# Spatial-reduction attention with a mixture of adapters: gated activations of 27 chunks turned by DMA, query columns in another order

## The chip, the cores and the metric

The kernel runs on one core of a Trainium2 chip. The metric is the device time of one execution in microseconds. A core has five engines that run side by side and wait for each other by semaphores: TensorE (PE in the profile; its weight loads are PEld), VectorE (DVE), ScalarE (ACT), GpSimd (POOL) and SyncE (SP). SyncE does no arithmetic here: it issues DMAs, one after the other, and waits before each for what that DMA needs. Casting DMAs are issued by GpSimd. Each engine works through its own instructions in program order, so an instruction that waits holds up all that follow on its engine.

## The reference

Queries `q` (4 batches of 12288 rows of 128 channels) attend to keys that are averages of 4 x 4 patches of `kv`, so 768 keys a batch, and keys and values are the same. Each output row then goes through 2 of 8 rank-16 adapters.

```python
kv_pool = kv.reshape(B, H // r, r, W // r, r, C).mean(axis=(2, 4))
kv_flat = kv_pool.reshape(B, -1, C) @ w_sr
k = v = kv_flat
s = scale * (q @ k.transpose(0, 2, 1))
a = np.exp(s - s.max(-1, keepdims=True))
a /= a.sum(-1, keepdims=True) + 1e-09
x = a @ v
...
logits = x @ w_gate
topk = np.argpartition(-logits, K, axis=1)[:, :K]   # K = 2
...
out = x + sum over the two chosen experts e of  w_e * ((x @ A[e]) @ B[e])
```

The second softmax is over the two chosen logits. The kernel computes all eight adapters at once as one 128 x 128 down-projection (8 experts of rank 16), multiplies the 128 activations by the gate of their expert, and applies one 128 x 128 up-projection.

## The kernel before

**Chunks and slots.** The 49152 queries are cut into 96 chunks of 512 (24 a batch), each of four pieces of 128 rows. Four chunks form a group. The first chunks are ordered by a list written out by hand (`opening`). From `k = 8` on a Python loop writes one slot per pass (line 547), and `keep` holds every engine to that order. In slot k from 13 on TensorE does three score pairs (`unit` calls `scores`) for chunk k and the attention of chunk k - 1, while chunk k - 2 is normalised. An older chunk goes through the adapters: it enters in some slot t (`enter[t]`; `kx`) with its transposes and down-projection, has its gated activations turned one slot later (`kh`), and gets its up-projection and its result two slots after it entered (`ku`).

**A slot on TensorE,** in order: the first score pair; `transposes`, which turns the four pieces of normalised rows of the entering chunk (`xn`) and the four pieces of gated activations of the chunk before (`hg`) into one PSUM tile `tt_ps`; the second pair; `up` (`d_ps`) of the chunk that is two slots on; six attention matmuls of the first piece (`acc`); the third pair; `down` (`h_ps`); in some slots (`rest`) a step of the next batch's keys and values (`kpT_ps`, `v_ps`, `kfT_ps`); 18 attention matmuls of the three other pieces.

**VectorE in a slot:** reciprocal of the softmax sums (`rinv`), normalisation (`xn`), copy of `tt_ps` to `tts`, sum of up-projection and rows (`osb`), `max` for the routing, gating (`gate`, writes `hg`), and the copies of `rest`. ScalarE takes the exponential of each score pair (`em`) and a tanh for the gates. GpSimd computes the gates (`over`, `gw`), adds up the patches of the next batch (`kvr`) and issues the casts of the queries.

**Buffers.** PSUM has eight banks. `ps_s` has two tiles of two banks for the score pairs, `ps_a` one tile of two banks for the attention, `ps_m` two tiles of one bank, which `tt_ps`, `d_ps`, `h_ps` and the tiles of `rest` take in turn. A tile is given out again when everything that reads its last contents is done. In SBUF, `xn` has a ring of six pairs of chunks, results eight buffers (`osb`), `tts` and `hg` three each.

**Queries.** From group 2 on GpSimd casts a group to bf16 in DRAM (`cast_q`), and SyncE loads it transposed (`load_qT`), group g in slot 4g - 6 for most. Row 16p + j of a group sits in partition p of the output; the transposed group has columns in the order (j, p), so that chunk m of a group is the j from 4m to 4m + 3. Groups 0 and 1 are turned by TensorE (`turn_q`).

**The last part.** The chunks from `TURN` = 68 up to `SOLO` = 90 (`by_dma`) have both their normalised rows and their gated activations turned by DMA from SyncE (`narrow`, `strip`, `turn_dma`), without TensorE; the last six chunks stand in a tail written out by hand.

Of the kernel before, what the change touches and what calls it, by code (L numbers as in the profile page):

```python
# [11 lines left out]
BF16 = mybir.dt.bfloat16  # L12
U16 = mybir.dt.uint16
FP16 = mybir.dt.float16
AF = mybir.ActivationFunctionType
# [5 lines left out]
def kernel(  # L21
# [10 lines left out]
    nc = tc.nc  # L32
    P = 128
    B, N, C = q.tensor.shape
# [20 lines left out]
    ppool = ctx.enter_context(tc.tile_pool(name="ppool", bufs=8))  # L55
    xpool = ctx.enter_context(tc.tile_pool(name="xpool", bufs=1))
    rpool = ctx.enter_context(tc.tile_pool(name="rpool", bufs=4))
    gpool = ctx.enter_context(tc.tile_pool(name="gpool", bufs=6))
    run = ctx.enter_context(tc.tile_pool(name="run", bufs=3))
    opool = ctx.enter_context(tc.tile_pool(name="opool", bufs=8))  # L60
    qdram = ctx.enter_context(tc.tile_pool(name="qdram", bufs=1, space=bass.MemoryType.DRAM))
    ps_s = ctx.enter_context(tc.tile_pool(name="ps_s", bufs=2, space=bass.MemoryType.PSUM))
# [3 lines left out]
    keep = tc.keep_in_program_order  # L66

    def mm(*a, **k):
        return keep(nc.tensor.matmul(*a, **k))  # L69
# [5 lines left out]
    NG = N // GT  # L75
    q_bf, qT, kvr, spare = {}, {}, {}, {}

    def cast_q(g):
        t = qdram.tile([GT, C], BF16, tag=f"q{g}", name=f"qbf{g}")
        keep(nc.gpsimd.dma_start(t, q[g // NG, (g % NG) * GT:(g % NG + 1) * GT]))  # L80
        q_bf[g] = t

    def load_qT(g):
        if g < B * NG - GC:
            t = qpool.tile([P, GT], BF16, tag="qT", name="qT")
        else:
            if "q" not in spare:
                spare["q"] = kvpool.tile([P, 4, 2, 4 * C], FP32, tag="kvr", name="qTs")
            t = spare["q"][:, g % GC].rearrange("p x c -> p (x c)").bitcast(BF16)
        keep(nc.sync.dma_start(t.rearrange("c (j p) -> c j p", p=P),  # L90
                               q_bf[g].rearrange("(p j) c -> p (j c)", p=P), transpose=True))
        qT[g] = t


# [191 lines left out]
    def scores(k, r):  # L286
        b = k // NB
        if k not in em:
            em[k] = ppool.tile([P, J, T], FP16, tag="em", name="em")
        rhs = qT[k // GC][:, (k % GC) * T:(k % GC + 1) * T]  # L290
        ps = ps_s.tile([P, 2, T], FP32, tag="sg", name="sg")
        for i in range(2):
            mm(ps[:, i], kfT[b][:, 2 * r + i], rhs, start=True, stop=True)
        keep(nc.scalar.activation(em[k][:, 2 * r:2 * r + 2], ps, AF.Exp, bias=0.0, scale=scale))  # L294

    def attend(k, s):
        b = k // NB
        if s == 0:
            acc[k] = ps_a.tile([P, S, 256], FP32, tag="acc", name="acc")
        o = acc[k][:, s, 0:VE]  # L300
        for j in range(J):
            mm(o, em[k][:, j, s * P:(s + 1) * P], vx[b][:, j, 0:VE], start=(j == 0),
               stop=(j == J - 1))

    def attend_part(k, r):
        if r == 0:
            acc[k] = ps_a.tile([P, S, 256], FP32, tag="acc", name="acc")
        for s in range(S):
            for j in (2 * r, 2 * r + 1):
                mm(acc[k][:, s, 0:VE], em[k][:, j, s * P:(s + 1) * P], vx[k // NB][:, j, 0:VE],  # L310
                   start=(j == 0 and s % 2 == 0), stop=(j == J - 1 and s % 2 == 1))

    def normalize(k):
# [91 lines left out]
    def turn_dma(t, *what):  # L405
# [3 lines left out]
        for i, (d, k) in enumerate(what):  # L409
            d[k] = strip(t, 1)[:, lo + i]  # L410

    def down(k):
        hp[k] = mtile([P, S, P], name="h_ps")
        for s in range(S):
            mm(hp[k][:, s], xT[k][:, s], a_bf, start=(s == 0), stop=(s == S - 1))

    def gate(k, into=None):
        k0, m = first[k], k - first[k]
        hg[k] = run.tile([P, S, P], BF16, tag="hg", name="hg") if into is None else into
        keep(nc.vector.tensor_tensor(  # L420
            hg[k].rearrange("p s (e r) -> p (s e) r", e=E),
            hp[k].rearrange("p s (e r) -> p (s e) r", e=E),
            gw[k0][:, m * S:(m + 1) * S].rearrange("p s e -> p (s e)")
            .unsqueeze(2).broadcast_to([P, S * E, RK]), op=ALU.mult))

    def up(k):
        dp[k] = mtile([P, S, C], name="d_ps")
        for s in range(S):
            mm(dp[k][:, s], hgT[k][:, s], b_bf, start=(s == 0), stop=(s == S - 1))

    def finish(k):
        osb = opool.tile([P, S, C], FP32, tag="osb", name="osb")
        keep(nc.vector.tensor_tensor(osb, dp[k], xn[k][:, :, 0:C], op=ALU.add))  # L433
        keep(nc.sync.dma_start(
            out[k // GC * GT:(k // GC + 1) * GT].rearrange("(p j) c -> p j c", p=P)
            [:, k % GC * S:(k % GC + 1) * S], osb))
        for d in (em, acc, xn, xT, hgT, hp, hg, dp):
            d.pop(k, None)

# [25 lines left out]
    loads.update({61: 20, 63: 21, 64: 18, 65: 22, 66: 19, 67: 23})  # L465
    assert len(casts) == B * NG - 4

    def begin(k):
        nonlocal sums, rest
        b, i = divmod(k, NB)  # L470
        g = k // GC
        if k in loads:
            load_qT(loads[k])
        if k in casts:
            cast_q(4 + casts.index(k))
        if b + 1 < B:
            lo = 3 if b == 0 else 0
            if i == lo:
                sums, rest = prepare(b + 1, nc.gpsimd)
                sums = sum(sums, [])  # L480
            if lo <= i < 12 + lo:
                load_kv(b + 1, (i - lo) // 4, (i - lo) % 4, None)
        if k == 7:
            for _ in range(2):
                sums.pop(0)()
# [12 lines left out]
    while left:  # L498
        can = [k for k in left if ready[k] <= t]
        enter[t] = can[:2] if t == SOLO + 2 else can[:1]  # L500
        left = [k for k in left if k not in enter[t]]
        t += 1

    kh, ku, kd, kdone = [], [], [], []
    engines = {"DVE": nc.vector, "ACT": nc.scalar, "POOL": nc.gpsimd}
# [41 lines left out]
    for k in range(k1, NCHUNK):  # L547
        b, i = divmod(k, NB)
        ka = att.get(k, [])
        kx = enter.get(k, [])  # L550
        begin(k)

        def after_norm(kn):
            top(kn)
# [2 lines left out]

        kn = [n for n in att.get(k - 1, []) if normed[n] == k]
        unit()
        if kx and not kd and all(x_ in by_dma for x_ in kx):  # L560
            down(kx[0])
            todo = []
            for n in kn:
                normalize(n)
                if n in by_dma:
                    narrow(n, k)
                    todo = [(xT, n)]
            tanhs()
# [22 lines left out]
            kh, ku = kx, kh  # L591
            continue
        tanhs()
        for x_ in kd:
# [1 line left out]
        for n in kn:  # L596
            normalize(n)
            if n in by_dma:
                narrow(n, k)
                turn_dma(k, (xT, n))  # L600
        px, ph = ([c for c in ks if c not in by_dma] for ks in (kx, kh))
        pairs = [(px[j] if j < len(px) else None, ph[j] if j < len(ph) else None)
                 for j in range(max(len(px), len(ph)))]
        for x_, h_ in pairs[:1]:
# [71 lines left out]
    def part(k, o, js):  # L676
        for s in range(S):
            for j in js:
                mm(o[:, s, 0:VE], em[k][:, j, s * P:(s + 1) * P], vx[k // NB][:, j, 0:VE],
                   start=(j == 0 and s % 2 == 0), stop=(j == J - 1 and s % 2 == 1))  # L680

    def wide(o):
# [9 lines left out]
        for s in range(S):  # L692
            mm(o[:, s], hgT[k][:, s], b_bf, start=(s == 0), stop=(s == S - 1))

    def dest(k):
        return out[k // GC * GT:(k // GC + 1) * GT].rearrange("(p j) c -> p j c", p=P)[
            :, k % GC * S:(k % GC + 1) * S]

    def add_here(k, lo, hi, queue):
        osb = opool.tile([P, S, C], FP32, tag="osb", name="osb")[:, 0:hi - lo]  # L700
        keep(nc.vector.tensor_tensor(osb, dp[k][:, lo:hi], xn[k][:, lo:hi, 0:C], op=ALU.add))
        keep(queue.dma_start(dest(k)[:, lo:hi], osb))

    def carry(k):
        osb = opool.tile([P, S, C], FP32, tag="osb", name="osb")
# [2 lines left out]

    def add_there(k):
        keep(nc.gpsimd.tensor_tensor(dp[k], dp[k], xn[k][:, :, 0:C], op=ALU.add))  # L710
        keep(nc.sync.dma_start(dest(k), dp[k]))

    def gate_part(k, lo, hi):
        if lo == 0:
# [116 lines left out]
```

## Time and profile before

| | |
|---|---|
| time, median of 3 runs | 380.78 us (380.48 to 381.1) |
| span of the profiled execution | 379.1 us |
| VectorE busy | 307.6 us |
| GpSimd busy | 217.8 us |
| exponentials (L294), 288 of 128 x 1024 | 1022 ns each |
| gatings (L420), 71 into `hg` and 22 into `turn` | 691 and 680 ns each |
| copies of `tt_ps` (L389), 68 of 1024 elements and 5 of 512 | 691 and 416 ns each |
| turned by DMA: query groups / chunks of the last part | 22 / 23 DMAs |

The profile is one execution; its span is from the first to the last instruction, and the device time holds a little more than that. No other time of the profiled execution is shown beside its span. In rows of the timeline stand the start, the duration, the engine, the line, the operation, what is written and read, the count, and in brackets how long the engine had been idle and who released it. A row of several matmuls lasts from the first start to the last end; since matmuls overlap in the array, the distance from one row's start to the next row's start is what a piece of TensorE work takes. All matmuls have line 69, a helper's, so they are told apart by their tiles. In the table of waits stand the waiting engine, its tile and line, the releaser, and the total in us, the count and the longest. In the view by windows each engine's busy time in a stretch stands with its number of instructions, then the granted clock, the DMA engines' busy share and their GB/s.

### The profile page before, as it was taken

The numbers are of one execution on the slowest core, as the hardware profiler recorded it, in microseconds if no ns is written. First come the engines' busy times: TensorE is split into PE (matmuls) and PEld (weight loads), VectorE is DVE, ScalarE is ACT, GpSimd is POOL, SyncE is SP. The second block draws the span as 40 slices with busy tenths as digits, with TensorE's granted clock in tenths as the row PEclk, the third lists the DMA queues.
The fourth block names the chain that finished last, engine by engine and source line by source line (L and its number), as shares of the span: only waits on it lengthen the run. The fifth ranks groups of instructions, "written<-read, shape, count | busy, mean of one in ns | idle before, by whom it ended". The sixth has DMA issues, their size and how long they took to land.

```text
span 379.1 us, 11473 instructions
## 1 busy us (share of the span) xinstructions
PE 368.8 (97%) x4448; PEld 292.5 (77%) x4448; DVE 307.6 (81%) x925; ACT 293.3 (77%) x368; POOL 217.8 (57%) x493
## 2 busy tenths in 40 slices
PE   8899999999999999999999999999999999999993
PEld 5577788788788887878788887878787777777782
DVE  1447799998989889898989888898988777777785
ACT  1448986776878788787878787777778999999873
POOL 0120468878732387777833267777675666666442
PEclk9999999999999999999999999999999999999998
DMA  7988979999999998997898998989955867777623
GB/s 247 388 291 151 279 184 266 340 224 241 152 213 228 299 278 268 255 235 165 171 201 226 288 239 245 306 233 198 217 137 140 169 163 153 150 205 168 141 86 140
DMA packets 93863, 82.22 MB, mean 217 GB/s; under 512 B 73104, under 2 KB 73872, under 8 KB 93456
## 3 DMA queue, kind: packets, MB, share of 16 engines
q1 hardware_dynamic: 92672, 69.75, 69.8%
q0 software_dynamic: 704, 11.54, 17.0%
q8 instruction: 35, 0.57, 0.6%
q10 hardware_dynamic: 432, 0.20, 0.2%
q14 instruction: 20, 0.16, 0.2%
HBM read 50.53 MB, written 36.70 MB: 230 GB/s over the span
## 4 chain that ended last, share of the span: by engine, by line
PE 91%; DMA 4%; DVE 2%; issue 1%; ACT 1%; SPq 0%; POOL 0%; ACTq 0%; DVEq 0%; POOLq 0%
PE acc L69 35%; PE sg L69 32%; PE tt_ps L69 8%; PE d_ps L69 5%; PE h_ps L69 5%; DMA kvr<-in_kv_dram 4%; PE kpT_ps L69 2%; PE v_ps L69 1%; DVE kvr L135 1%; DVE xn L320 1%; PE kfT_ps L69 1%; DMA out_dram<-osb 1%; PE qT_ps L69 0%; SPq L102 0%; PE tail_ps L69 0%
## 5 line engine op out<-in xcount | busy, mean ns | idle before, releaser
L294 ACT ACTIVATE em<-sg 128x1024 f16<-128x1024 f32 x288 | 282.4, 1022 | 66.8 <-PE sg L69 64.1
L69 PE MATMUL acc<-vx,em 128*128 128x136 f16 x2280 | 166.5, 223 | 0.0
L69 PEld LDWEIGHTS <-em 128*128 128x128 f16 x2304 | 145.2, 98 | 7.7 <-DVE xn L320 0.4
L69 PE MATMUL sg<-qT,kfT 128*128 128x512 bf16 x480 | 142.1, 379 | 0.8 <-ACT em L294 0.7
L320 DVE TENSOR_TENSOR xn<-acc,rinv 128x540 f32<-128x540 f32 x95 | 68.4, 720 | 3.3
L69 PEld LDWEIGHTS <-tts 128*128 128x128 bf16 x564 | 43.0, 98 | 31.6 <-issue 0.4
L223 POOL TENSOR_TENSOR kvr<-kvr 128x512 f32<-128x512 f32 x54 | 67.3, 1270 | 0.1
L352 POOL TENSOR_TENSOR over<-xn,srt 128x64 f32<-128x64 f32 (+1 forms) x120 | 30.9, 278 | 55.4 <-DVE srt L340 55.3
L433 DVE TENSOR_TENSOR osb<-d_ps,xn 128x512 f32<-128x512 f32 x91 | 62.5, 688 | 0.0
L420 DVE TENSOR_TENSOR hg<-h_ps,gw 128x512 bf16<-128x512 f32 x71 | 49.0, 691 | 6.3 <-POOL gw L368 1.2
L389 DVE COPY tts<-tt_ps 128x1024 bf16<-128x1024 bf16 (+1 forms) x73 | 49.0, 672 | 0.0
L69 PEld LDWEIGHTS <-kfT 128*128 128x128 bf16 x576 | 45.3, 98 | 2.7 <-issue 1.0
L315 DVE RECIPROCAL rinv<-acc 128x4 f32<-128x4 f32 x95 | 17.3, 182 | 36.9 <-PE acc L69 35.9
L367 POOL TENSOR_TENSOR gw<-th,over 128x64 f32<-128x64 f32 (+1 forms) x60 | 17.3, 288 | 49.6 <-ACT th L365 47.4
L69 PEld LDWEIGHTS <-xn 128*128 128x128 bf16 x296 | 22.5, 98 | 16.7 <-DVE xn L320 0.4
L340 DVE MAX8 srt<-xn 128x8 f32<-128x8 f32 x380 | 34.4, 152 | 0.1
L69 PE MATMUL sg<-qTs,kfT 128*128 128x512 bf16 x96 | 28.6, 379 | 0.0
L69 PE MATMUL tt_ps<-id_bf,xn 128*128 128x128 bf16 x284 | 27.4, 219 | 0.0
L69 PE MATMUL h_ps<-a_bf,tts 128*128 128x128 bf16 x284 | 27.4, 219 | 0.0
L69 PE MATMUL tt_ps<-id_bf,hg 128*128 128x128 bf16 x280 | 27.1, 219 | 0.0
L69 PE MATMUL d_ps<-b_bf,tts 128*128 128x128 bf16 x276 | 26.7, 219 | 0.1
L358 POOL TENSOR_SCALAR over<-over 128x64 f32<-128x64 f32 (+1 forms) x60 | 19.8, 330 | 5.4
(93 smaller groups left out, 280.7 us busy)
## 6 DMA issues: line engine op xcount, KB each, us to landing
out_dram<-osb SPq DMA_DIRECT2D x94, 256.0 KB, 4.3
kvr<-in_kv_dram SPq DMA_DIRECT2D x45, 512.0 KB, 7.8
qbf<-in_q_dram POOLq DMA_DIRECT2D x22, 512.0 KB, 7.7
qf<-in_q_dram SPq DMA_DIRECT2D x8, 256.0 KB, 7.4
kvr<-in_kv_dram SPq DMA_DIRECT2D x6, 256.0 KB, 7.8
out_dram<-osb SPq DMA_DIRECT2D x3, 128.0 KB, 2.3
turn<-turn SPq DMA_TRANSPOSE x23, 3.1
qT<-qbf SPq DMA_TRANSPOSE x18, 7.4
```

The source lines that it names most:

```text
L69: return keep(nc.tensor.matmul(*a, **k))
L223: keep(adder.tensor_tensor(u[:, lo:hi], u[:, lo:hi], v[:, lo:hi], op=ALU.add))
L294: keep(nc.scalar.activation(em[k][:, 2 * r:2 * r + 2], ps, AF.Exp, bias=0.0, scale=scale))
L315: keep(nc.vector.reciprocal(ri, acc[k][:, :, VC]))
L320: keep(nc.vector.tensor_tensor(x[:, :, 0:VC], acc[k][:, :, 0:VC], ri.unsqueeze(2).broadcast_to([P, S, VC]), op=ALU.mult))
L340: keep(nc.vector.max(srt[k0][:, m, s], xn[k][:, s, C:C + E]))
L352: keep(eng.tensor_tensor(d, lg, so[:, :, i].unsqueeze(2).broadcast_to([P, n, 8]), op=ALU.subtract))
L358: keep(eng.tensor_scalar(mask, mask, 0.0, None, op0=ALU.is_ge))
L367: keep(eng.tensor_tensor(w[:, 0:n], th, mask, op=ALU.mult))
L389: keep(nc.vector.tensor_copy(sb[:, lo:hi], ps[:, lo:hi]))
L420: keep(nc.vector.tensor_tensor(hg[k].rearrange("p s (e r) -> p (s e) r", e=E), hp[k].rearrange("p s (e r) -> p (s e) r", e=E), gw[k0][:, m ...
L433: keep(nc.vector.tensor_tensor(osb, dp[k], xn[k][:, :, 0:C], op=ALU.add))
```

## The change

Three things are changed together.

1. **Query order.** The cast writes a group as 16 rows; row r holds, for each of 8 blocks u, sixteen query rows one after the other (4 KB runs in bf16). The DMA transpose then turns a 16-row matrix, and the columns of the transposed group come in the order (u, j, r), with p = 16u + r. A chunk's 512 columns are thus no longer one run: the moving operand of a score matmul takes 8 runs of 64. This holds for groups from 2 on.
2. **Layout of the exponentials.** `em` is laid out by piece, then key block, then row. One ScalarE instruction reads the 1024 scores in 64 runs of 16 (in groups 0 and 1 in 8 runs of 128) and writes four runs of 256. The weights of an attention matmul are still 128 neighbouring elements.
3. **Turned by DMA.** The chunks that enter in slots 15 to 23, 36 to 47 and 60 to 65 (`by_queue`, 27 chunks) are gated into a tile of their own (`hs`, four buffers), turned by a DMA from SyncE into `ht` (six buffers), and get their up-projection five slots after they entered (`late_up`), behind that of a chunk that takes the usual way where there is one. In the slot after such a chunk entered, `tt_ps` has its four `xn` transposes alone and the copy 512 elements. A group's query load is issued after the first score pair, or behind the turning DMA, and no longer at the slot's start.

```diff
+    hpool = ctx.enter_context(tc.tile_pool(name="hpool", bufs=4))
...
     def cast_q(g):
-        t = qdram.tile([GT, C], BF16, tag=f"q{g}", name=f"qbf{g}")
-        keep(nc.gpsimd.dma_start(t, q[g // NG, (g % NG) * GT:(g % NG + 1) * GT]))
+        t = qdram.tile([16, GT // 16 * C], BF16, tag=f"q{g}", name=f"qbf{g}")
+        src = q[g // NG, (g % NG) * GT:(g % NG + 1) * GT]
+        keep(nc.gpsimd.dma_start(t.rearrange("r (u x) -> r u x", u=8),
+                                 src.rearrange("(u r x) c -> r u (x c)", r=16, u=8)))
         q_bf[g] = t
...
-        keep(nc.sync.dma_start(t.rearrange("c (j p) -> c j p", p=P),
-                               q_bf[g].rearrange("(p j) c -> p (j c)", p=P), transpose=True))
+        keep(nc.sync.dma_start(t.rearrange("c (i r) -> c i r", r=16), q_bf[g], transpose=True))
...
     def scores(k, r):
...
-            em[k] = ppool.tile([P, J, T], FP16, tag="em", name="em")
+            em[k] = ppool.tile([P, S, J, P], FP16, tag="em", name="em")
         rhs = qT[k // GC][:, (k % GC) * T:(k % GC + 1) * T]
+        if k // GC > 1:
+            rhs = qT[k // GC].rearrange("c (u m x) -> c m u x", u=8, m=GC)[:, k % GC]
...
-        keep(nc.scalar.activation(em[k][:, 2 * r:2 * r + 2], ps, AF.Exp, bias=0.0, scale=scale))
+        o = em[k][:, :, 2 * r:2 * r + 2]
+        if k // GC > 1:
+            o = o.rearrange("p s i (u r) -> p s (i u) r", r=16)
+            i_ = ps.rearrange("p i (u s r) -> p s (i u) r", s=S, r=16)
+        else:
+            i_ = ps.rearrange("p i (s t) -> p s i t", s=S)
+        keep(nc.scalar.activation(o, i_, AF.Exp, bias=0.0, scale=scale))
...
-            mm(o, em[k][:, j, s * P:(s + 1) * P], vx[b][:, j, 0:VE], start=(j == 0),
+            mm(o, em[k][:, s, j], vx[b][:, j, 0:VE], start=(j == 0),
...
+    def turn_h_dma(k):
+        hgT[k] = hpool.tile([P, S, P], BF16, tag="ht", name="ht", bufs=6)
+        keep(nc.sync.dma_start(hgT[k].rearrange("c s p -> c s p"),
+                               hg[k].rearrange("p s c -> p (s c)"), transpose=True))
...
+    by_queue = [k for t in range(15, TURN - 2) if t < 24 or t % NB >= 12 for k in enter[t]]
+    late_up = {}
...
-        begin(k)
+        begin(k, False)
...
         unit()
+        if k in loads and not any(x_ in by_queue for x_ in kx):
+            load_qT(loads[k])
+        ku = ku + late_up.pop(k, [])
...
-        px, ph = ([c for c in ks if c not in by_dma] for ks in (kx, kh))
+        px = [c for c in kx if c not in by_dma]
+        ph = [c for c in kh if c not in by_dma and c not in by_queue]
...
         for x_ in kx[:1]:
             down(x_)
-            gate(x_)
+            if x_ in by_queue:
+                gate(x_, hpool.tile([P, S, P], BF16, tag="hs", name="hs"))
+                turn_h_dma(x_)
+                late_up[k + 5] = [x_]
+                if k in loads:
+                    load_qT(loads[k])
+            else:
+                gate(x_)
...
-        ku = kh
+        ku = [c for c in kh if c not in by_queue]
```

The other lines give the stores a helper (`store`) of their own and index `em` in its new layout; neither changes an instruction's count.

More of the change, by code (lines that the diff above doesn't have):

```diff
@@ L309, in attend_part @@
             for j in (2 * r, 2 * r + 1):
-                mm(acc[k][:, s, 0:VE], em[k][:, j, s * P:(s + 1) * P], vx[k // NB][:, j, 0:VE],
+                mm(acc[k][:, s, 0:VE], em[k][:, s, j], vx[k // NB][:, j, 0:VE],
                    start=(j == 0 and s % 2 == 0), stop=(j == J - 1 and s % 2 == 1))
@@ L429, in up, with store @@
             mm(dp[k][:, s], hgT[k][:, s], b_bf, start=(s == 0), stop=(s == S - 1))
+    def store(queue, k, osb, lo=0, hi=S):
+        to = out[k // GC * GT:(k // GC + 1) * GT].rearrange("(p j) c -> p j c", p=P)
+        keep(queue.dma_start(to[:, k % GC * S + lo:k % GC * S + hi], osb))
     def finish(k):
@@ L433, in finish @@
         keep(nc.vector.tensor_tensor(osb, dp[k], xn[k][:, :, 0:C], op=ALU.add))
-        keep(nc.sync.dma_start(
-            out[k // GC * GT:(k // GC + 1) * GT].rearrange("(p j) c -> p j c", p=P)
-            [:, k % GC * S:(k % GC + 1) * S], osb))
+        store(nc.sync, k, osb)
         for d in (em, acc, xn, xT, hgT, hp, hg, dp):
@@ L466, with begin @@
     assert len(casts) == B * NG - 4
-    def begin(k):
+    def begin(k, queries=True):
         nonlocal sums, rest
@@ L471, in begin @@
         g = k // GC
-        if k in loads:
+        if k in loads and queries:
             load_qT(loads[k])
@@ L590 @@
             attend(ka[0], 3)
-            kh, ku = kx, kh
+            kh, ku = kx, [c for c in kh if c not in by_queue]
             continue
@@ L678, in part @@
             for j in js:
-                mm(o[:, s, 0:VE], em[k][:, j, s * P:(s + 1) * P], vx[k // NB][:, j, 0:VE],
+                mm(o[:, s, 0:VE], em[k][:, s, j], vx[k // NB][:, j, 0:VE],
                    start=(j == 0 and s % 2 == 0), stop=(j == J - 1 and s % 2 == 1))
@@ L693, in up_into @@
             mm(o[:, s], hgT[k][:, s], b_bf, start=(s == 0), stop=(s == S - 1))
-    def dest(k):
-        return out[k // GC * GT:(k // GC + 1) * GT].rearrange("(p j) c -> p j c", p=P)[
-            :, k % GC * S:(k % GC + 1) * S]
     def add_here(k, lo, hi, queue):
@@ L701, in add_here @@
         keep(nc.vector.tensor_tensor(osb, dp[k][:, lo:hi], xn[k][:, lo:hi, 0:C], op=ALU.add))
-        keep(queue.dma_start(dest(k)[:, lo:hi], osb))
+        store(queue, k, osb, lo, hi)
     def carry(k):
@@ L710, in add_there @@
         keep(nc.gpsimd.tensor_tensor(dp[k], dp[k], xn[k][:, :, 0:C], op=ALU.add))
-        keep(nc.sync.dma_start(dest(k), dp[k]))
+        store(nc.sync, k, dp[k])
     def gate_part(k, lo, hi):
```

## The prediction

> **What bounds the kernel now.** I read the page first, then the table of waits, then one slot (one pass of the main loop, one chunk of 512 queries) in order of time.
>
> ```profile
> span 379.1 us, 11473 instructions
> PE 368.8 (97%) x4448; PEld 292.5 (77%) x4448; DVE 307.6 (81%) x925; ACT 293.3 (77%) x368; POOL 217.8 (57%) x493
> PE 91%; DMA 4%; DVE 2%; issue 1%; ACT 1%; SPq 0%; POOL 0%; ACTq 0%; DVEq 0%; POOLq 0%
> ACT em L294 <- PE sg L69: 64.1, 78, 3.3
> PE sg L69 <- ACT em L294: 0.7, 1, 0.7
> ```
>
> TensorE is busy for 97% and holds 91% of the chain that ended last. The exponentials wait for its score matmuls (64.1 us in 78 waits), the reverse happened once. The next view gives the busy time of each engine in the slots that the change touches (16-24, 37-48, 61-66).
>
> ```profile
> core 0: us, PE busy (x) PEld busy (x) DVE busy (x) ACT busy (x) POOL busy (x), PEclk, DMA share, GB/s
> 78.50:112.90 34.40, 34.40 (x435) 27.86 (x433) 30.90 (x90) 26.35 (x32) 22.49 (x42) 1.00 1.02 216
> 157.00:202.10 45.10, 45.10 (x573) 36.52 (x571) 40.57 (x118) 34.96 (x42) 30.48 (x56) 1.00 0.90 194
> 246.20:268.70 22.50, 22.50 (x287) 18.22 (x285) 20.18 (x59) 17.55 (x21) 16.17 (x28) 1.00 0.98 211
> ```
>
> TensorE has no gap there, at full granted clock, so every matmul removed counts, until some other wait ends last. Which one, the timeline of slot 50 tells:
>
> ```profile
> 205.76 0.59 PE L69 MATMUL sg<-qT,kfT 128*128 128x512 bf16 x2
> 206.19 0.39 PE L69 MATMUL tt_ps<-id_bf,xn 128*128 128x128 bf16 x4
> 206.42 0.39 PE L69 MATMUL tt_ps<-id_bf,hg 128*128 128x128 bf16 x4
> 206.46 1.02 ACT L294 ACTIVATE em<-sg 128x1024 f16<-128x1024 f32 x1 [0.75 <-PE sg L69]
> 206.64 0.59 PE L69 MATMUL sg<-qT,kfT 128*128 128x512 bf16 x2
> 206.84 0.69 DVE L389 COPY tts<-tt_ps 128x1024 bf16<-128x1024 bf16 x1
> 207.07 0.39 PE L69 MATMUL d_ps<-b_bf,tts 128*128 128x128 bf16 x4
> 207.30 0.52 PE L69 MATMUL acc<-vx,em 128*128 128x136 f16 x6
> 207.65 0.59 PE L69 MATMUL sg<-qT,kfT 128*128 128x512 bf16 x2
> 209.37 0.59 PE L69 MATMUL sg<-qT,kfT 128*128 128x512 bf16 x2
> ```
>
> Start to start, the slot is 209.37 - 205.76 = 3.61 us. Four transposes of the gated activations take 206.64 - 206.42 = 0.22, an up-projection 207.30 - 207.07 = 0.23. There are two score tiles (`ps_s`, two buffers), so the third score pair (207.65) may start only when the slot's first exponential has read its tile: 206.46 + 1.02 = 207.48. It clears that by 0.17. What the release itself takes shows in slot 70, where the first exponential was late:
>
> ```profile
> 280.89 1.02 ACT L294 ACTIVATE em<-sg 128x1024 f16<-128x1024 f32 x1 [1.31 <-PE sg L69]
> 281.97 0.59 PE L69 MATMUL sg<-qT,kfT 128*128 128x512 bf16 x2
> ```
>
> It ended at 281.91 and the pair started 0.06 later: this is the one wait of the table above. So a plain slot has 0.17 - 0.06 = 0.11 us to spare between first and third score pair, and everything that the change removes (transposes) or moves (up-projections) stands between these two.
>
> **The change part by part.** *Transposes.* 27 slots lose the four matmuls of `hg`: 27 x 0.22 = 5.9 us of TensorE work, all of it ahead of the third score pair. The first exponential starts when the first pair is done, as before, so only 0.11 of the 0.22 shortens the slot; TensorE waits out the other 0.11. In nine of the 27 (17-19, 38-40, 62-64) the up-projection has moved away too, 0.45 is gone ahead of that pair, and still the slot gains 0.11 alone, with 0.34 of waiting. Gain: 27 x 0.11 = 3.0.
>
> *Up-projections five slots on.* In the changed program's order of TensorE instructions the nine come back in slots 26-28, 50-52 and 68-70, each of which still has its own and all eight transposes. Each costs 0.23 again. It also allocates a fourth tile in a pool of two PSUM buffers (`ps_m`): transposes, first up, second up, down. The second up takes the transposes' buffer, so it waits for VectorE's copy of it, which ended at 206.84 + 0.69 = 207.53 in slot 50. How soon TensorE follows VectorE:
>
> ```profile
> 369.10 0.72 DVE L320 TENSOR_TENSOR xn<-sg,rinv 128x540 f32<-128x540 f32 x1
> 369.88 0.40 PE L69 MATMUL tail_ps<-id_bf,xn 128*128 128x128 bf16 x4 [0.21 <-DVE xn L320]
> ```
>
> 369.88 - 369.82 = 0.06. So the second up starts at 207.59 instead of 207.30, and attention, the third scores and the down-projection queue behind it on TensorE: 0.23 + 0.29 = 0.52 a slot, 9 x 0.52 = 4.7 lost. The slot's third score pair is then late enough for its exponential, so that wait adds nothing there.
>
> *GpSimd's chain.* In slots 18-21 and 44-45 the pooling of the next batch already ends last:
>
> ```profile
> 87.81 0.32 POOL L367 TENSOR_TENSOR gw<-th,over 128x64 f32<-128x64 f32 x1 [1.41 <-ACT th L365]
> 93.39 0.58 POOL L80 DMA_DIRECT2D qbf<-in_q_dram  x1
> 98.01 2.07 POOL L221 TENSOR_TENSOR kvr<-kvr 128x512 f32<-128x512 f32 x2
> 99.81 0.39 PE L69 MATMUL h_ps<-a_bf,tts 128*128 128x128 bf16 x4
> 100.14 0.44 PE L69 MATMUL kpT_ps<-id_f,kvr 128*128 128x128 f32 x2
> 187.23 2.08 POOL L221 TENSOR_TENSOR kvr<-kvr 128x512 f32<-128x512 f32 x2
> 189.37 0.44 PE L69 MATMUL kpT_ps<-id_f,kvr 128*128 128x128 f32 x2
> ```
>
> After 87.81 GpSimd shows no idle until the last sum ends at 100.08, and `kpT_ps` follows at 100.14, where the down-projection before it, at 0.23 like an up-projection, was over by 100.04. In slot 45 it is 189.31 and 189.37. What slots 18-21 and 44-45 gain ahead of that is waited out: 6 x 0.11 = 0.7 lost. The two casts inside the first chain become 128 pieces instead of 16. At 0.58 each they add nothing, at eight times 0.58 they add 8.1 us; I take 0.58, as SyncE issues a store of 128 pieces (one per partition) in 0.53, a row shown below under DMA and the nearest one.
>
> *Exponentials.* They read the scores in 64 runs of 16 and write 4 runs of 256. No strided read by ScalarE is in the trace. The nearest rows:
>
> ```profile
> L294 ACT ACTIVATE em<-sg 128x1024 f16<-128x1024 f32 x288 | 282.4, 1022 | 66.8 <-PE sg L69 64.1
> L706 ACT COPY osb<-acc 128x512 f32<-128x512 f32 x1 | 0.6, 597 | 0.0
> L320 DVE TENSOR_TENSOR xn<-acc,rinv 128x540 f32<-128x540 f32 x95 | 68.4, 720 | 3.3
> L433 DVE TENSOR_TENSOR osb<-d_ps,xn 128x512 f32<-128x512 f32 x91 | 62.5, 688 | 0.0
> ```
>
> VectorE's `xn` reads PSUM in 4 runs and takes 720 ns for 540 elements against 688 for 512, 32 ns for 28 elements: about one step each, so the runs are free. Lower bound 0 (a shorter one than one run of 1024 is excluded). Upper bound one step per run: (1022 - 597)/512 = 0.83 ns, x 63 = 52 ns. I take 0.
>
> *Scores.* The moving operand comes in 8 runs of 64. A pair takes 0.43 (206.64 to 207.07), so a column 0.42 ns; between 0 and one column per run: 7 x 0.42 = 2.9 ns on 88 x 6 matmuls, 1.6 us. I take 0, as the `xn` row does. A gain is excluded: columns are as many. Here the Trainium skill speaks against the change: "PSUM — Partial Sum Buffer", Specifications, gives 8-byte cachelines in PSUM and says that any non-contiguous access pattern slows matmuls significantly. The matmul's output stays one run of 512, it is the two reads that are broken up, and no run here shows such a read. Were the rule to hold for them, the forecast would be that of rival B.
>
> *DMA.* 27 transposes of 128 KB more, 23 like them exist, and query transposes of another shape, all issued on SyncE.
>
> ```profile
> turn<-turn SPq DMA_TRANSPOSE x23, 3.1
> qT<-qbf SPq DMA_TRANSPOSE x18, 7.4
> 245.12 7.70 SPq L90 DMA_TRANSPOSE qTs<-qbf  x1
> 252.91 0.53 SPq L434 DMA_DIRECT2D out_dram<-osb  x1
> 293.39 1.24 SPq L407 DMA_TRANSPOSE turn<-turn  x1
> ```
>
> A turned activation lands in about 3.1 us and is used five slots on, over 17 us after slot start; a query group is loaded six slots (21 us) ahead and lands in 7.4. Issue costs 27 x 1.24 = 33 us of SyncE, whose queue waits for each gate; behind it stand the stores (8 buffers) and, outside the key-load slots, query loads. Cover: these 14 us of lead; without it TensorE would wait at the up-projection. VectorE's shorter copy saves time on an engine that is not the bound.
>
> **Sum**, against the profile's own span: -3.0 + 4.7 + 0.7 = +2.4 us, 379.1 to 381.5. The timed runs stand 380.78 - 379.1 = 1.7 above that span; with it 383.1, 0.6% slower.
>
> **The rivals.**
> A: the exponential pays one step per run. Each of the 27 slots waits 0.05 longer, 27 x 0.05 = 1.4: 384.5. For it: no such read in the trace; against: the `xn` row.
> B: the runs slow the score matmuls, +1.6 on TensorE: 384.7.
> C: SyncE or the DMA engines fall behind. For it: DMA is at 0.90 to 1.02 in these slots, and a query transpose held SyncE for 7.70 us; slots 61-66 add 6 x 1.24 = 7.4 us of issue. Against: 14 us of lead. If slots 68-70 waited 1 us each: 386.1.
> D: neither buffer wait binds. Then the whole 5.9 us comes off and the moved projections cancel: 374.9. Against it stand slot 70's wait and the two-buffer pools; it decides if the first exponential were released 0.34 us earlier than 207.48.
> E: the second up finds a free buffer; then nine slots cost 0.23 alone: -3.0 + 2.1 + 0.7 = -0.2, 380.6.
> F: the casts take 1 us longer each on GpSimd; slots 19 and 20 hold two, +2: 385.1.
> On the skill's side, "TensorE: Matmul & The Clock Gate", Back-to-back issue gap, gives about 81 ns a matmul at 128 columns in such a stream; 108 of them would be an estimated 8.7 us under rival D. Slot 50 has 0.22 for four, so the trace disagrees and decides.
>
> **How the numbers follow.** Forecast 0.52, A 0.12, B 0.05, C 0.08, F 0.05, D 0.07, E 0.11. A measurement of this kernel can tell 0.2% (0.76 us) from no change. Faster, 0.12: D and 0.05 from E and the forecast, should the gain per slot be larger. Within 0.2%, 0.13: most of E and the forecast's edge. Slower, 0.75. The range 380.0 to 386.3 leaves out D and the far ends of C and F; the forecast's own is 381.8 to 384.0.
>
> **What would show it.** Right: in slots 17-24 the third score pair starts 0.06 after the first exponential's end, TensorE with gaps of about 0.1 and 0.34 and slots of 3.50; in 26-28 and 50-52 the second up starts just after the copy of the transposes, slots of 4.13; unchanged exponentials (1.02), score pairs (0.43), and casts (0.58). Wrong: reduced slots of 3.39 or less, double slots of 3.84, or TensorE waiting for DMA at an up-projection.

## The result and the profile after

The changed kernel takes 385.56 us (median of 383.38, 383.59, 387.53 and 388.08), the kernel before 380.84 us in the same comparison: 1.0134 times as long, 95% interval 1.0097 to 1.0172. Executions more than 1.5% above the quickest of their kernel (among them five of the 61 of the kernel before, up to 433 us) are left out of all ratios here.

The four times are not one cluster but two pairs, 4 us apart. The profiled execution belongs to the upper pair (387.53 us, span 385.7). From its page, the head, the busy times, the DMA packets and the chain that ended last by engine:

```profile
span 385.7 us, 11315 instructions
...
PE 369.4 (96%) x4334; PEld 287.5 (75%) x4340; DVE 299.2 (78%) x925; ACT 294.7 (76%) x368; POOL 218.6 (57%) x493
...
DMA packets 66311, 85.75 MB, mean 222 GB/s; under 512 B 42736, under 2 KB 43504, under 8 KB 65904
...
PE 78%; DMA 7%; DVE 6%; POOL 3%; ACT 2%; issue 2%; SPq 0%; ACTq 0%; DVEq 0%; POOLq 0%
```

TensorE's share of the chain fell from 91% to 78%; that of DMA rose from 4% to 7%, that of VectorE from 2% to 6%. The table of waits of the same execution shows where:

```profile
ACT em L304 <- PE sg L70: 67.6, 85, 3.3
...
DVE hs L435 <- DMA ht<-hs: 4.6, 2, 3.4
...
PE tt_ps L70 <- DVE hs L435: 2.6, 2, 2.5
...
PE sg L70 <- ACT em L304: 0.7, 1, 0.7
```

The second and third row did not exist before: a gating on VectorE waited 3.4 us for a transposing DMA, and TensorE 2.5 us for that gating. Both are in slot 47. (The other wait of the second row, 1.1 us, is in slot 43; slots 43 to 45 together lose only 0.1 us by it.) The timeline around slot 47, and ahead of it the gating of slot 43:

```profile
182.60 0.69 DVE L435 TENSOR_TENSOR hs<-h_ps,gw 128x512 bf16<-128x512 f32 x1 [1.13 <-DMA ht<-hs]
...
183.65 8.20 SPq L93 DMA_TRANSPOSE qT<-qbf  x1
192.56 2.01 SPq L424 DMA_TRANSPOSE ht<-hs  x1
195.28 1.25 SPq L424 DMA_TRANSPOSE ht<-hs  x1
197.27 1.90 SPq L424 DMA_TRANSPOSE ht<-hs  x1
...
198.00 0.10 PEld L70 LDWEIGHTS <-xn 128*128 128x128 bf16 x1
199.87 1.31 SPq L424 DMA_TRANSPOSE ht<-hs  x1
200.11 0.69 DVE L435 TENSOR_TENSOR hs<-h_ps,gw 128x512 bf16<-128x512 f32 x1 [3.44 <-DMA ht<-hs]
200.85 0.38 PE L70 MATMUL tt_ps<-id_bf,xn 128*128 128x128 bf16 x4 [2.48 <-DVE hs L435]
```

The gating needs one of four `hs` buffers, and a buffer is free only when the DMA that turns it has read it. The buffer is that of slot 43, filled at 183.29: its DMA was issued only at 192.56, behind a query load that held SyncE for 8.20 us, and had read it by 200.1. The gating holds `h_ps` in `ps_m`, so the transposes of the next slot got no tile, and TensorE stood still.

A second execution of the same kernel, profiled later beside the experiments, took 383.56 us and has no such wait; there the DMA of slot 43 was issued at 186.57. Slot lengths are read from one start of `xn` on VectorE to the next. All stretches of the span, in us:

| slots | before | after, 387.53 us | after, 383.56 us | forecast | measured (383.56) |
|---|---|---|---|---|---|
| up to 15 | 78.90 | 78.30 | 78.96 | 0 | +0.06 |
| 16-24 | 34.45 | 33.77 | 33.82 | -0.55 | -0.63 |
| 26-28, double | 10.83 | 12.36 | 12.35 | +1.56 | +1.52 |
| 37-48 | 45.19 | 48.36 | 43.94 | -1.10 | -1.25 |
| 50-52, double | 10.83 | 12.35 | 12.35 | +1.56 | +1.52 |
| 61-67 | 26.22 | 25.48 | 25.48 | -0.66 | -0.74 |
| 68-70, double | 11.78 | 13.30 | 13.30 | +1.56 | +1.52 |
| all others | 148.56 | 148.59 | 148.57 | 0 | +0.01 |
| from the last `xn<-acc` on | 12.36 | 13.18 | 13.04 | 0 | +0.68 |
| span | 379.1 | 385.7 | 381.8 | +2.4 | +2.7 |

Two things made the time: the prices that the forecast names, paid by every execution, and a backlog of transposes that costs 4.4 us in slots 37-48 and that some executions have.

The two forecast waits, in the timeline of the first trace, slots 39 and 51:

```profile
164.73 0.72 DVE L330 TENSOR_TENSOR xn<-acc,rinv 128x540 f32<-128x540 f32 x1
164.97 0.59 PE L70 MATMUL sg<-qT,kfT 128*128 128x512 bf16 x2
165.00 2.85 ACT L304 ACTIVATE em<-sg 128x1024 f16<-128x1024 f32 x3 [0.49 <-PE sg L70]
165.51 0.53 PE L70 MATMUL acc<-vx,em 128*128 128x136 f16 x6
166.08 0.59 PE L70 MATMUL sg<-qT,kfT 128*128 128x512 bf16 x2
...
214.43 0.69 DVE L399 COPY tts<-tt_ps 128x1024 bf16<-128x1024 bf16 x1
214.66 0.39 PE L70 MATMUL d_ps<-b_bf,tts 128*128 128x128 bf16 x4
215.18 0.38 PE L70 MATMUL d_ps<-b_bf,ht 128*128 128x128 bf16 x4
215.40 0.52 PE L70 MATMUL acc<-vx,em 128*128 128x136 f16 x6
```

In slot 39 the first of three exponentials, at 1.02, ends at 166.02, and the third pair starts at 166.08, 0.06 later, although the attention ahead of it was over (165.51 and the 0.35 us of such a piece). In the trace of 383.56 us the third pair follows the exponential by 0.05 to 0.06 in 26 of the 27 reduced slots, and the second up-projection follows the copy by as much in all nine double slots. In slot 51 the copy ends at 215.12 and the second up-projection starts at 215.18, though the first one was done at 214.89. From there on the slot is 215.40 instead of 214.89, 0.51 us late.

### The profile page after: what moved, and what is told of

It reads as the page before. It is cut to its first block, busy times and chain, and to the rows that moved or that the text cites. A ratio compares the mean times of both kernels' runs of the same rounds, so it can differ in the third digit from the quotient of the medians.

```text
span 385.7 us, 11315 instructions
## 1 busy us (share of the span) xinstructions
PE 369.4 (96%) x4334; PEld 287.5 (75%) x4340; DVE 299.2 (78%) x925; ACT 294.7 (76%) x368; POOL 218.6 (57%) x493
## 2 busy tenths in 40 slices
DMA packets 66311, 85.75 MB, mean 222 GB/s; under 512 B 42736, under 2 KB 43504, under 8 KB 65904
## 4 chain that ended last, share of the span: by engine, by line
PE 78%; DMA 7%; DVE 6%; POOL 3%; ACT 2%; issue 2%; SPq 0%; ACTq 0%; DVEq 0%; POOLq 0%
PE acc L70 32%; PE sg L70 26%; DMA ht<-hs 6%; PE d_ps L70 5%; PE tt_ps L70 5%; PE h_ps L70 5%; PE kpT_ps L70 2%; DVE xn L330 2%; DVE tts L399 2%; DMA kvr<-in_kv_dram 2%; ACT em L304 1%; POOL kvr L225 1%; PE v_ps L70 1%; PE qT_ps L70 1%; DVE rinv L325 1%
## 5 line engine op out<-in xcount | busy, mean ns | idle before, releaser
L304 ACT ACTIVATE em<-sg 128x1024 f16<-128x1024 f32 x288 | 283.7, 1023 | 71.6 <-PE sg L70 67.6
L452 DVE TENSOR_TENSOR osb<-d_ps,xn 128x512 f32<-128x512 f32 x91 | 61.7, 687 | 0.6
L70 PEld LDWEIGHTS <-tts 128*128 128x128 bf16 x456 | 34.8, 98 | 25.7 <-issue 0.9
L70 PEld LDWEIGHTS <-kfT 128*128 128x128 bf16 x576 | 46.3, 98 | 4.9 <-issue 2.3
L399 DVE COPY tts<-tt_ps 128x1024 bf16<-128x1024 bf16 (+1 forms) x73 | 41.6, 570 | 0.0
L435 DVE TENSOR_TENSOR hg<-h_ps,gw 128x512 bf16<-128x512 f32 x44 | 30.4, 691 | 3.9 <-POOL gw L378 1.2
L435 DVE TENSOR_TENSOR hs<-h_ps,gw 128x512 bf16<-128x512 f32 x27 | 18.7, 692 | 16.8 <-POOL gw L378 7.6
L70 PEld LDWEIGHTS <-turn 128*128 128x128 bf16 x176 | 13.4, 98 | 10.2 <-DMA turn<-turn 0.5
```

Of the source, the lines that this page charges most:

```text
L304: keep(nc.scalar.activation(o, i_, AF.Exp, bias=0.0, scale=scale))
L399: keep(nc.vector.tensor_copy(sb[:, lo:hi], ps[:, lo:hi]))
L435: keep(nc.vector.tensor_tensor(hg[k].rearrange("p s (e r) -> p (s e) r", e=E), hp[k].rearrange("p s (e r) -> p (s e) r", e=E), gw[k0][:, m ...
```

## The experiments

**Room for the backlog.** Eight `hs` buffers instead of four, paid for with one exponential buffer.

```diff
-    hpool = ctx.enter_context(tc.tile_pool(name="hpool", bufs=4))
+    hpool = ctx.enter_context(tc.tile_pool(name="hpool", bufs=8))
-    ppool = ctx.enter_context(tc.tile_pool(name="ppool", bufs=8))
+    ppool = ctx.enter_context(tc.tile_pool(name="ppool", bufs=7))
```

> The changed kernel with eight instead of four buffers for the gated tile (hs); em gets seven instead of eight buffers to make room. Theory (the gate of slot 47 waits for its buffer, whose turning DMA stands behind a query load on SyncE): the 3.44 us wait of VectorE is gone, slots 47 and 48 take 3.60 and 3.48 instead of 6.52 and 4.89, reduced slots stay at 3.48 and double slots at 4.12, and the time is 383.4 us in every run. Rival (the DMAs themselves are too late and the wait only moves on to the up-projection): 385 to 388, with TensorE waiting for ht.

Measured: median 386.77 us, 1.0144 (1.0104 to 1.0183) times the kernel before. Two executions at 383.5 and 383.7, three at 385.8, 387.8 and 387.9, one at 404.1. The profiled one (383.51) has no stretched slot. So four buffers are where the backlog shows in the first trace, but more of them don't remove it; where the late executions waited no trace shows.

**The order and the layout alone.** No activation turned by DMA; queries, scores and exponentials as in the changed kernel.

```diff
-    by_queue = [k for t in range(15, TURN - 2) if t < 24 or t % NB >= 12 for k in enter[t]]
+    by_queue = []
```

> Query order and layout of the exponentials alone, no chunk turned by the new DMA (by_queue empty). Theory (reads in runs of 16 and 64 are free): 380.8 us, the same as before, exponentials 1.02, plain slots 3.61. Rival A (a step per run on ScalarE): exponentials of 1.07, the time hardly moves since a plain slot has 0.11 to spare. Rival B (runs slow the score matmuls): 382.4, slots of 3.63.

Measured: 380.75 us (380.36 to 381.21, 11 executions), 1.001 (1.0 to 1.002). The 64 runs of 16, the 8 runs of 64 and the casts in 128 pieces together cost 0.8 us (0.2%) at most. The DMA packets fell from 93863 to 51623 for the same 82.22 MB, which by itself gained nothing.

**The turned activations alone,** with the queries, the scores and the exponentials' reads as before.

```diff
-        t = qdram.tile([16, GT // 16 * C], BF16, tag=f"q{g}", name=f"qbf{g}")
+        t = qdram.tile([GT, C], BF16, tag=f"q{g}", name=f"qbf{g}")
...
-        keep(nc.sync.dma_start(t.rearrange("c (i r) -> c i r", r=16), q_bf[g], transpose=True))
+        keep(nc.sync.dma_start(t.rearrange("c (j p) -> c j p", p=P),
+                               q_bf[g].rearrange("(p j) c -> p (j c)", p=P), transpose=True))
```

> The turning by DMA and the late up-projections alone, with the query groups cast and turned as before (128 rows) and scores in one run of 512. Theory (the shape of the query transpose is not what makes SyncE late): the same two levels as the changed kernel, 383.4 to 388, double slots 4.12. Rival (the 16-row transposes hold SyncE longer): 383.4 in every run, no wait for an hs buffer.

Measured: 383.16 us in one execution, 406.66 to 425.76 in five: neither the theory's 383.4 to 388 nor the rival's 383.4. The run was repeated on another chip.

> Once more the turned activations alone, with the query transposes, the scores' single run and the memory order of before. Theory (query transposes of the old shape, 93863 packets in the kernel before, leave no room on the DMA engines for 27 more): most executions are late by 10 us or more, TensorE waiting at attention and up-projection for ht and qT, as on the first chip. Rival (that chip was disturbed, and the shape of the query transposes hardly matters): 383.2 in most executions, as its quickest one was.

Measured: 392.69 to 415.15 us, median 401.71; the ratio of the two quickest is 1.0363 (1.0325 to 1.0401). The theory held: with the old query transposes every execution is late here, and 11 of the 12 on both chips. From the page of the execution of 392.69 us, then its slot 40:

```profile
DMA packets 108551, 85.75 MB, mean 219 GB/s; under 512 B 87792, under 2 KB 88560, under 8 KB 108144
```

```profile
168.81 8.92 SPq L417 DMA_TRANSPOSE ht<-hs  x2
171.04 0.50 PE L70 MATMUL sg<-qT,kfT 128*128 128x512 bf16 x1 [3.51 <-DMA qT<-qbf]
...
179.31 0.69 DVE L428 TENSOR_TENSOR hs<-h_ps,gw 128x512 bf16<-128x512 f32 x1 [6.18 <-DMA ht<-hs]
180.06 0.38 PE L70 MATMUL d_ps<-b_bf,ht 128*128 128x128 bf16 x4 [2.93 <-DVE hs L428]
```

The bytes are those of the changed kernel, 85.75 MB, but in 108551 packets instead of 66311. TensorE waits here for a query group and for the same `hs` ring.

**The second up-projection later,** behind the first attention piece, with the buffers of the first experiment.

```diff
-        ku = ku + late_up.pop(k, [])
+        kl = late_up.pop(k, [])
...
             attend(ka[0], 0)
+        for u_ in kl:
+            up(u_)
+            finish(u_)
```

> As e1_hs8, and the late up-projection stands behind the first attention piece instead of ahead of it. Theory (in a double slot the second up waits 0.29 us for the copy of the transposes): the attention piece of 0.35 us covers that wait, double slots take 3.84 instead of 4.12, 9 x 0.29 = 2.6 us less than e1_hs8, 380.8 us. Rival (two up-projections are too much for VectorE in one slot, or the tile pool holds it up elsewhere): double slots stay near 4.1 and the time at 383.4.

Measured: 384.88 to 385.45 us in three executions, 1.013 (1.0111 to 1.0148). The trace is of a fourth, at 406.08 us; only its slots without a wait for a DMA are read. Double slots 26 and 27 fell from 4.12 to 3.83, as expected. But the edit also moved the late up-projection in slots that have only this one, and there slots 22 and 23 went from 4.00 and 3.60 to 4.36 and 3.91. The result is 1.7 us worse than the changed kernel's quick executions. Where the single ones lose 0.3 the trace shows in slot 23:

```profile
107.21 0.69 DVE L452 TENSOR_TENSOR osb<-d_ps,xn 128x512 f32<-128x512 f32 x1 [0.52 <-PE d_ps L70]
107.44 0.39 PE L70 MATMUL h_ps<-a_bf,tts 128*128 128x128 bf16 x4
107.95 0.27 PE L70 MATMUL kfT_ps<-id_bf,vb 128*128 128x128 bf16 x2
```

The down-projection is done at 107.67 (107.44 + 0.23), but the step of `rest` takes the buffer of the late `d_ps` and starts at 107.95, 0.05 after the sum has read it (107.90): 0.28 us. Single slots without a step of `rest` keep their length (slot 24: 3.50). So the 0.3 is again a wait for one of the two buffers of `ps_m`.

**The changed kernel again,** and with a longer lead: up-projections eight slots on in the first two groups, with seven `hs` and nine `ht` buffers.

> The changed kernel as it is, to see how its time spreads beside the other three on one chip. Theory (two prices: 3.1 us that every execution pays in the reduced and double slots, and a backlog of transposes on SyncE and the DMA engines that only some executions pay): executions lie at 383.4 to 384, or 2 to 5 us above it, in no fixed share. Rival (there is one price, and the profiled execution with slots 47 and 48 at 6.52 and 4.89 us is the rule): executions within 1 us of each other, near 387.

Measured: 383.21 to 383.93 us five times and 388.94 once, 1.0103 (1.0064 to 1.0142). Two prices, in no fixed share.

```diff
-                late_up[k + 5] = [x_]
+                late_up[k + (8 if k < 60 else 5)] = [x_]
```

> Up-projections of the first two groups eight slots on instead of five, with room for seven activations before their transposes and nine behind them (4 and 6 before), paid for with one exponential buffer. Theory: the backlog of transposes is covered by 10 us more of lead, so no slot among 40 to 48 is stretched and executions lie within 1 us; but there are 15 double slots instead of 9 (26 to 31, 50 to 55, 68 to 70), each 0.52 us dearer than a plain one: 383.4 + 6 x 0.52 = 386.5. Rival (the lead was enough and the stretched slots come from the query loads, whatever the lead): the spread of the changed kernel stays, 386.5 to 390. Second rival (double slots cost only the 0.23 us of their projection, as the three that went elsewhere would say): 384.8.

Measured: 386.98 us (386.86 to 387.19), 1.0168 (1.0155 to 1.0182). No slot is stretched, slots 26 to 31 and 50 to 55 are all 4.12, and six double slots more cost 386.98 - 383.72 = 3.26 us, 0.54 each. The second rival's 0.23 is refuted.

**The third score pair later.** In the reduced slots a second attention piece stands ahead of it; all else as in the kernel with eight slots.

```diff
-        if k >= 13:
+        few = any(c in by_queue for c in kh)
+        if k >= 13 and few:
+            attend(ka[0], 1)
+            unit()
+            n0 = 2
+        elif k >= 13:
             unit()
             n0 = 1
```

> As the kernel with eight slots, and in the reduced slots a second attention piece stands ahead of the third score pair, so that the pair no longer waits for the slot's first exponential. Theory: what the transposes and projections gave up is now TensorE's own time: reduced slots without any up-projection (17 to 22, 38 to 43, 62 to 64) go from 3.48 to about 3.16 where GpSimd's sums don't hold them (11 of 15), those with one from 3.48 to 3.39: 11 x 0.32 + 9 x 0.09 = 4.3 less, 382.2. Rival (something other than the first exponential holds the reduced slots at 3.48, ScalarE's or VectorE's own pace): slots stay at 3.48, 386.5.

Measured: 383.96 us (383.46 to 384.2), 1.0086 (1.0073 to 1.0099): 3.0 less where 4.3 were expected. Slots with an up-projection went to 3.39, those without only to 3.28. What holds them there is in the next trace.

**Both waits taken away:** in addition the second up-projection of the double slots, and only there, stands behind the first attention piece.

> As the one before, and in the double slots the second up-projection stands behind the first attention piece, when VectorE has copied the transposes and the buffer is free. Theory: double slots 3.84 instead of 4.12: 13 x 0.29 = 3.8 less (69 and 70 have other holds), 378.4, under the kernel before. Rival (the wait for the buffer only moves on, to the down-projection that takes the next one): double slots stay at 4.12, 382.2.

Measured: 380.38 us (379.77 to 380.95, 11 executions), 0.999 (0.9979 to 1.0). Double slots 3.83, 3.6 us less. From its timeline, double slot 50:

```profile
204.47 0.69 DVE L399 COPY tts<-tt_ps 128x1024 bf16<-128x1024 bf16 x1
204.70 0.39 PE L70 MATMUL d_ps<-b_bf,tts 128*128 128x128 bf16 x4
204.92 0.52 PE L70 MATMUL acc<-vx,em 128*128 128x136 f16 x6
205.28 0.39 PE L70 MATMUL d_ps<-b_bf,ht 128*128 128x128 bf16 x4
205.50 0.59 PE L70 MATMUL sg<-qT,kfT 128*128 128x512 bf16 x2
```

The copy ends at 205.16, before the second up-projection (205.28) wants its tile; it now costs 0.22 and no wait. Reduced slot 38 of the same trace:

```profile
161.19 0.72 DVE L330 TENSOR_TENSOR xn<-acc,rinv 128x540 f32<-128x540 f32 x1
161.21 0.39 PE L70 MATMUL tt_ps<-id_bf,xn 128*128 128x128 bf16 x4
161.43 0.59 PE L70 MATMUL sg<-qT,kfT 128*128 128x512 bf16 x2
161.97 0.88 PE L70 MATMUL acc<-vx,em 128*128 128x136 f16 x12
```

The second pair is done at 161.86 (161.43 + 0.43), and the attention starts at 161.97, 0.06 after the normalisation (161.91) has read the one accumulator of `ps_a`. That is the next wait, 0.11 us of the missing 0.12. It stood in the changed kernel already, hidden by the wait for the exponential: in slot 39 above the second pair is done at 165.40, and the attention starts at 165.51, 0.06 after the normalisation (165.45). Against the kernel before, the reduced stretches give 5.6 us (slots 16-24 1.2, 37-48 2.7, 61-67 1.7), and the 15 double slots take 3.9 back. Slot 72 takes 0.76, where TensorE waits for a turned chunk of the last part, the closing 0.6 and the opening 0.2.

**The order on SyncE.** The changed kernel with each query load ahead of the slot's turned activations.

```diff
-        if k in loads and not any(x_ in by_queue for x_ in kx):
+        if k in loads:
             load_qT(loads[k])
...
                 late_up[k + 5] = [x_]
-                if k in loads:
-                    load_qT(loads[k])
```

> The changed kernel with each query load ahead of the slot's turned activations on SyncE, at the start of the slot, instead of behind them. Theory (the stretched slots come from SyncE's order: a query transpose holds the queue for 1.2 to 8.2 us, and the transposes that empty the four hs buffers stand behind it): slots 20, 24, 40, 44, 48 and 63 to 66 are stretched in most executions, 387 to 391. Rival (the backlog is one of the DMA engines alone, and the order on SyncE doesn't matter): as the changed kernel, 383.4 to 384 in most executions.

Measured: 383.11 to 383.83 us four times and 390.81 once, 1.0076 (1.0063 to 1.0089). The theory failed; the rival's number came. As far as five executions tell, who stands first on SyncE does not decide.

**One group only.** The kernel without both waits, but only slots 36 to 47 turned by DMA, five and eight slots on.

```diff
+    by_queue = [k for t in range(36, 48) for k in enter[t]]
```

> Only the second group (slots 36 to 47) turned by DMA, five slots on, with the attention piece ahead of the third score pair and the second up-projection behind the first attention piece. Theory: in the trace with eight slots this group's stretch, slots 37 to 55, took 69.10 us against 70.44 before; three double slots fewer give 3 x 0.22 and three reduced slots get their projection back, 3 x 0.11: 380.7 - 1.3 - 0.7 + 0.3 = 379.0, in some executions up to 4 us more where transposes pile up. Rival (GpSimd's sums or the one accumulator buffer take it back): 380.4 or more.

Measured: 379.89 us (379.26 to 381.74, 12 executions), 0.9988 (0.9975 to 1.0001); 379.0 was expected. It is the lowest median of all the kernels, 0.8 us below the kernel before (380.69), and the interval still touches no change.

> As the one before, eight slots on instead of five. Theory: 380.7 - 1.3 = 379.4, executions within 1 us of each other. Rival (the lead of eight slots was not what kept executions together): some executions 2 to 4 us later.

Measured: seven of twelve executions at 379.06 to 380.46 us, four at 383.4 to 387.7 and one, the profiled one, at 976.56, in which plain slots take 9.74 us; 0.9993 (0.9972 to 1.0014). The expected narrow spread did not come, so the eight slots' lead is not shown to be the remedy. No trace shows where the four late ones waited.

## Why the prediction was right, and where not

**The number.** The forecast of 383.1 us is 2.5 below the measured median, which lies inside the stated range but where no execution was: two of the four stood near the forecast, two 4 us above it. In the repeat five of six stood near it and the median was 383.72. Where a median of four falls is thus in part luck; the mechanism has to be judged by the slots.

**The reduced slots.** Right: 3.48 where 3.50 was forecast, and the third pair 0.06 behind the exponential. In slot 39, without up-projection, TensorE waits 0.33 us where 0.34 was forecast, but in two places: 0.11 ahead of the attention, for the accumulator, and 0.22 ahead of the third pair. The forecast did not name the first. Taking the wait for the exponential away brought the reduced slots to 3.39 and 3.28.

**The double slots.** Right: 4.12 where 4.13 was forecast, with the second up-projection 0.06 behind the copy. Six more of them cost 0.54 each, and with the wait gone the price is 0.22. Slots 69 and 70 have other lengths (4.48 and 4.71), but the three together give the forecast's price to 0.04.

**GpSimd's chain.** Right: slots 18 to 21 take 15.72 us in the quick trace (85.97 to 101.69, from `xn` to `xn`) and 15.67 before (86.22 to 101.89); nothing was gained there.

**Exponentials, scores, casts.** Right to take 0. Rivals B (1.6 us) and F (2 us) fall with the run of the order alone, whose interval ends at 0.8. Rival A falls with the exponential's own duration, as that run has no reduced slots in which a longer one would show in the time; it has 1023 ns in the page after:

```profile
L304 ACT ACTIVATE em<-sg 128x1024 f16<-128x1024 f32 x288 | 283.7, 1023 | 71.6 <-PE sg L70 67.6 <-remote 0.9 <-PE acc L70 0.3
```

A cast's issue on GpSimd takes 0.60 us (median) instead of 0.58.

The rule of the Trainium skill ("PSUM — Partial Sum Buffer", Specifications), that any non-contiguous access pattern slows matmuls significantly, does not show here where ScalarE reads PSUM in 64 runs; the matmul's own output stayed one run.

**DMA.** This is the step that failed: "Cover: these 14 us of lead". In the quick executions the lead covers the transposes, and their 383.2 to 383.9 us stand 0.1 to 0.8 above the forecast of 383.1. In others the cover was not enough: the profiled one lost 2.92 us in slot 47 (6.52 instead of 3.60) and 1.41 in slot 48. That is rival C's kind, but not its place: no up-projection waited. The ring of four `hs` buffers ran out first, which the forecast did not cost, though four slots are less than the lead of five. The DMA issues of the first and of the second trace, 164 to 194 us:

```profile
ht<-hs SPq DMA_TRANSPOSE x6, 11.2
qT<-qbf SPq DMA_TRANSPOSE x2, 12.4
```

```profile
ht<-hs SPq DMA_TRANSPOSE x8, 7.4
qT<-qbf SPq DMA_TRANSPOSE x2, 11.8
```

A turned activation landed in 11.2 us (median) in the late execution and in 7.4 in the quick one, where the forecast had 3.1 from transposes in a calmer part of the kernel. In the late one the buffer of slot 43 was free only 16.8 us after it was filled (183.29 to 200.1), and for 9.3 of these its DMA stood waiting on SyncE. What tips an execution stays open. Eight `hs` buffers and the other order on SyncE still had late executions. The longer lead had none in three kernels (20 executions), but some in a fourth; and those three ran in one comparison, in which the kernel before had no late execution either, so the lead is not shown to be the reason. With the old shape of the query transposes 11 of 12 executions were late.

**The closing.** The forecast had nothing there; 0.7 and 0.8 us more pass from the last `xn<-acc` to the end in the two traces of the changed kernel. The last VectorE operation of the trace before, then that of the trace after:

```profile
375.24 0.42 DVE L701 TENSOR_TENSOR osb<-tail_ps,xn 128x256 f32<-128x256 f32 x1 [0.36 <-PE tail_ps L69]
```

```profile
381.11 0.42 DVE L728 TENSOR_TENSOR osb<-tail_ps,xn 128x256 f32<-128x256 f32 x1 [0.46 <-PE tail_ps L70]
```

From its end to the end of the span it is 379.1 - 375.66 = 3.4 us before and 385.7 - 381.53 = 4.2 after. With the order alone it is 3.2 and in the other kernels with `ht` 4.0 to 4.1 (3.3 in the execution of 976.56 us), so as far as these traces tell it goes with the turned activations and not with the query order. The cause was not tried.

**Rivals D and E.** With both waits removed the kernel came to 380.38 us, not to 374.9: the next waits (the accumulator, GpSimd's chain), the second up-projections' own time and a wait for a turned chunk took the rest. That E's 380.6 is close to it does not bear E out: E removes one wait, this kernel two, and it has 15 double slots instead of nine. E by itself was not run; in the run nearest to it, the second up-projection later, the single ones became slower too.

## What to carry to other kernels

Before taking matmuls out of a stage, look for the second wait that ends just before the first: here 0.11 us behind TensorE stood a score tile's release, so only half of the 0.22 us of removed work shortened a slot. Work moved to another slot is paid at that slot's price, and one more tile in a pool of two cost more there (0.29) than the work itself (0.22). A DMA that frees a buffer ring should be costed with its wait on the queue and its landing in that stretch of the kernel, not with its median elsewhere (3.1 us here, 7.4 and 11.2 where it was used); twice the buffers did not end the late executions.

## What the runs showed that was not expected

In these traces a stall of TensorE cost more than its length. Windows of the first trace, TensorE's busy time first and its granted clock in the column PEclk:

```profile
core 0: us, PE busy (x) PEld busy (x) DVE busy (x) ACT busy (x) POOL busy (x), PEclk, DMA share, GB/s
194.60:198.00 3.40, 3.40 (x45) 2.73 (x44) 2.02 (x7) 2.85 (x3) 1.08 (x4) 1.00 0.92 143
198.00:201.10 3.10, 0.62 (x7) 0.34 (x6) 0.98 (x3) 1.17 (x2) 1.35 (x4) 1.00 1.16 236
201.10:203.50 2.40, 2.39 (x21) 1.44 (x19) 1.93 (x7) 1.20 (x2) 0.00 (x0) 0.75 1.47 158
203.50:206.00 2.50, 2.50 (x23) 2.30 (x21) 0.88 (x2) 0.85 (x1) 0.00 (x0) 0.56 0.91 156
206.00:209.70 3.70, 3.70 (x49) 2.94 (x47) 3.24 (x10) 2.86 (x3) 1.12 (x4) 1.00 1.17 214
```

After 2.5 us of idleness the clock stood at 0.75 and 0.56 for some 5 us, and slot 48, in which TensorE was busy throughout, took 4.89 us instead of 3.48. So a third of the 4.3 us that slots 47 and 48 lost was paid after the stall was over. With the old query transposes it is the same: after 3.2 us of standing still the clock was 0.57 for 4 us.

```profile
167.80:171.00 3.20, 0.00 (x0) 0.00 (x0) 0.70 (x1) 0.00 (x0) 1.45 (x4) 1.00 1.30 379
171.00:175.00 4.00, 3.74 (x23) 2.40 (x25) 0.70 (x5) 2.40 (x4) 1.53 (x4) 0.57 0.70 161
```
